# Moving eight weight-difference instructions forward, and one block's second layer by one slot, in a fused gated-recurrence and maxout kernel

## The chip, the cores and the metric

The kernel runs on one core of one Trainium2 chip. Five engines work side by side, each with its own in-order instruction stream: PE (TensorE, matrix products), DVE (VectorE), ACT (ScalarE), POOL (GpSimd) and SP (which only issues transfers here). They wait for one another through semaphores. Time is the device time of one execution in microseconds (us). The kernel before takes 382.12 us, the median of 7 runs that lie between 382.0 and 382.54.

## The reference

Two stages are computed, one after the other. The first is a gated recurrence over 6144 time steps, for 4 batches and 256 channels. The second treats all 24576 tokens as rows and passes them through a layer of 1024 units, where each unit takes the larger of two products, and then through an output projection.

```python
sig = 1.0 / (1.0 + np.exp(-f_logit))
f = lower_bound + (1.0 - lower_bound) * sig
for t in range(S):
    h = f[:, t] * h + (1.0 - f[:, t]) * x[:, t]
    y[:, t] = h
tokens = y.reshape(B * S, D)                  # 24576 x 256
g = np.maximum(tokens @ w1, tokens @ w2)      # 24576 x 1024
out = g @ w_out                               # 24576 x 256
```

## The kernel before

**Algebra.** max(a, b) is written as a + ReLU(b - a). So with `wd` = w2 - w1 (scaled by the gate's factor) the first layer is ReLU(y @ wd), and the rest of the maximum, y @ w1 @ w_out, becomes one small extra product with `w13` = w1 @ w_out. The output is then ReLU(y wd) @ w_out + y @ w13: for each group of 128 tokens ten products, two with `w13` and eight with `wob` (w_out in fp16).

**Blocks and pairs.** Tokens are cut into 48 blocks of 512 time steps; two neighbouring blocks are a pair, so pair 2 is blocks 4 and 5 and pair 3 is blocks 6 and 7. For each block DVE computes the decay (`decay`, line 213), the drive (`drive`, line 223) and two scans along time (`scan`, line 230), one for each half of the channels; ACT computes the gate's sigmoid (`gate`, line 207, or `pair_gate`, line 285).

**First layer.** `first_layer(j, fc)` is two matrix products of 128x128 by 128x512 on PE (line 436) for one eighth of the hidden units. Two such calls, an even and an odd `fc`, fill one PSUM tile `dT`; the odd call is followed by one ReLU on ACT (line 444) that empties it into `r`. There are two `dT` tiles, so PE can be at most two of them ahead of ACT.

**Second layer, plain form.** Blocks 0 to 3 and the last two take `second_layer(j, slot)`: 40 products (line 482) for a block, issued in eight groups of five. After the groups 3 and 7 a PSUM tile is full and is copied out (line 496); for blocks 1 to 3 that copy is on DVE. After group 7 the store to memory is queued on SP (line 455).

**Second layer, seven products.** All other pairs use a scheme with seven products instead of eight for the two blocks of a pair (`sevenths`, matrix products on line 605). It needs four sums of ReLU tiles, made on DVE for each pair (`sum_of`, line 506: `sum3`, `sum1`, `sum2`, `sum4`), and four fixed differences of the weights, t1 to t4. `make_sevens` gives these as eight DVE subtractions (line 415): for each of t1, t3, t2, t4 in this order one of 128x512 from `wob` and one of 128x128 from `w13`.

**Order by hand.** The schedule is manual: the order of calls in the program is the order on every engine. Ahead of the main loop, blocks 0 to 3 are worked off in loops over `fc`. In the main loop each pair has 16 slots. A slot issues one `first_layer`, then (in pair 2 only) possibly one group of `second_layer(3, ...)`, then (from slot 2 of pair 3 on) a share of the queue of `sevenths` products of the pair before, then in slot 2 the transposing transfers of a later chunk (`cross`, SP and POOL), then in some slots a gate on ACT, and last those DVE steps of the list `seq` whose number is below 9 times (slot + 1). In pair 2 `seq` holds the two late scans of block 5 (27, 36), decay, drive and scans of block 6 (64 to 84), the eight subtractions (100 to 114), `sum3` (112), and decay and drive of block 7 (131, 133). In pair 3 it begins with `sum1` (9), `sum2` (18), the scans of block 7 (27, 36) and `sum4` (50).

**What the first products wait for.** In pair 3 the `sevenths` queue starts with 20 products that need only `r`, then 20 that read the result of `sum1` and t1, then 20 that read `sum2` and t2. The first layer of block 7, slot 8 of pair 3, needs the two scans of block 7.

Of the kernel before, what the change touches and what calls it, by code (L numbers as in the profile page):

```python
# [18 lines left out]
def kernel(  # L19
# [25 lines left out]
    for b in range(B):  # L45
# [3 lines left out]
        for nt in sizes:  # L49
            first = len(blocks)  # L50
# [45 lines left out]
    def fetch(c, s):  # L96
        b, t0, nt, _ = chunks[c]
        src = srcs[s][b, t0 : t0 + nt, :]
        if by_xbar(c, s):
            nc.gpsimd.dma_start(  # L100
                out=pieces(scratch[s][c % NSCR][:]), in_=pieces(src)
            )
        else:
            nat = inpool.tile([P, TB // P, D], HALF, name=("fT", "xT")[s])
            nc.gpsimd.dma_start(
                out=nat[:].rearrange("p i d -> p (i d)"),
                in_=src.rearrange("(p i) d -> p (i d)", p=P),
            )
            held[c, s] = nat
# [3 lines left out]
    def fetch_first(k):  # L113
        nt = TB // 2
        for s in range(2):
            raw = opool.tile([P, nt // P, D], FP32, name="osb")
            nc.sync.dma_start(
                out=raw[:],
                in_=srcs[s][0, k * nt : (k + 1) * nt, :].rearrange(
                    "(p i) d -> p i d", p=P  # L120
                ),
            )
            raws[k, s] = raw
# [215 lines left out]
    def fetch_w(g):  # L339
        cols = slice(g * DFF // NG, (g + 1) * DFF // NG)  # L340
        for w, src in ((w1n, moe_w1), (w2n, moe_w2)):
            nc.sync.dma_start(
                out=w[g][:],
                in_=src[:, cols].rearrange("(kc p) f -> p kc f", p=P),
            )

    def pool_waits(t):
        nc.gpsimd.tensor_copy(out=waited[:], in_=t)  # L348
# [56 lines left out]
    def right(k, cols):  # L405

        return wob[:, k * KH : (k + 1) * KH, cols], w13[:, k, cols]

    def make_sevens():
        b11, b12, b21, b22 = (right(k, c) for k in range(2) for c in (lo, hi))  # L410
        parts = [(t[:, 0:KH, :], t[:, KH, :]) for t in (t1, t2, t3, t4)]

        def minus(out, a, b):
            return [
                lambda q=q: nc.vector.tensor_tensor(  # L415
                    out=out[q], in0=a[q], in1=b[q], op=ALU.subtract
                )
                for q in range(2)
            ]

        return [
            *minus(parts[0], b12, b11),
            *minus(parts[2], b22, b12),
            *minus(parts[1], b22, parts[0]),
            *minus(parts[3], b21, parts[1]),
        ]
# [85 lines left out]
    def sum3(p):  # L512
        sum_of(p, 3, quarter(p, 0, 0), quarter(p, 1, 0), ALU.subtract)
# [105 lines left out]
    with tc.manual_schedule():  # L619
        nc.sync.dma_start(out=lbc[:], in_=lower_bound.rearrange("(h p) -> p h", p=P))  # L620
        nc.vector.tensor_copy(out=ident[:], in_=ident_f[:])
        nc.vector.tensor_scalar(
            out=om[:], in0=lbc[:], scalar1=-1.0, scalar2=1.0, op0=ALU.mult, op1=ALU.add
        )
        nc.vector.tensor_scalar_add(out=nom[:], in0=lbc[:], scalar1=-1.0)
        fetch_first(0)
        fetch_first(1)
        for g in range(NG):
            fetch_w(g)
        pool_waits(w1n[0][:, 0, 0:1])  # L630
        nc.gpsimd.dma_start(
            out=wob[:].rearrange("p (g q) c -> p g (q c)", g=NG),
            in_=moe_w_out.rearrange("(g p q) c -> p g (q c)", g=NG, q=NQ),
        )
        for c in range(1, 6):
            for s in range(2):
                fetch(c, s)
        nc.scalar.activation(out=warm[:], in_=om[:, 0:1], func=AF.Sigmoid)
        wt = ps_d.tile([P, 2, 2 * TB], HALF, name="dT")
        for q in range(8):  # L640
            nc.tensor.transpose(wt[:, 0, 0:P], ident[:], ident[:])
        first_bf16(0, 0, nc.vector.tensor_copy)
        first_bf16(0, 1, nc.vector.tensor_copy)
        first_turn(0)
        first_recurrence(0)
        first_bf16(1, 0, nc.scalar.copy)
        first_bf16(1, 1, nc.scalar.copy)
        first_turn(1)
        first_recurrence(1)
        for q in range(24):  # L650
            nc.tensor.transpose(wt[:, 0, 0:P], ident[:], ident[:])
        scale_w1(0)
        half_w1(0, nc.scalar.copy)
        make_wd(0)
        pt = turn_w1(0)
        keep_w1T(0, pt)
        scale_w1(1)
        for fc in range(4):
            first_layer(0, fc)
        half_w1(1, nc.vector.tensor_copy)  # L660
        make_wd(1)
        pt = turn_w1(1)
        for fc in range(4, 8):
            first_layer(0, fc)
        keep_w1T(1, pt)
        steps = turn_steps(1)
        make_w13(0)
        turn(steps[:8])
        gate(1)
        make_w13(1)  # L670
        turn(steps[8:])
        for step in scan_steps(1):
            step()
        cross(4, 5)
        for fc in range(FC):
            if fc == 4:
                turn(turn_steps(2))
                gate(2)
            second_layer(0, fc)
        for step in scan_steps(2):  # L680
            step()
        for fc in range(FC):
            first_layer(1, fc)
        turn(turn_steps(3))
        gate(3)
        early = scan_steps(3)
        for fc in range(FC):
            first_layer(2, fc)
            second_layer(1, fc)
            if fc < 4:  # L690
                early[fc]()
        cross(6)
        scans = {PAIR0: pair_scans(PAIR0)}
        gates = {0: 0, 1: 1, 4: 2, 5: 3}
        order = {
            2: ("decay0", "drive0"),
            3: ("scan00",),
            4: ("scan01",),
            6: ("decay1",),
            7: ("drive1",),  # L700
        }
        for fc in range(FC):
            first_layer(3, fc)
            second_layer(2, fc)
            if fc in gates:
                pair_gate(PAIR0, gates[fc])
            for t in order.get(fc, ()):
                scans[PAIR0][t]()

        queue, due = [], 0  # L710
        for p in range(PAIR0, NPAIR):
            first = p == PAIR0
            more = p + 1 < NPAIR
            seq = [(27, scans[p]["scan10"]), (36, scans[p]["scan11"])]
            if more:
                scans[p + 1] = pair_scans(p + 1)
                seq += [
                    (64, scans[p + 1]["decay0"]),
                    (66, scans[p + 1]["drive0"]),
                    (70, scans[p + 1]["scan00"]),  # L720
                    (84, scans[p + 1]["scan01"]),
                    (112, lambda: sum3(p)),
                    (131, scans[p + 1]["decay1"]),
                    (133, scans[p + 1]["drive1"]),
                ]
            if first:
                seq += [(100 + 2 * n, step) for n, step in enumerate(make_sevens())]
            else:
                seq += [
                    (9, lambda: sum1(p - 1)),  # L730
                    (18, lambda: sum2(p - 1)),
                    (50, lambda: sum4(p - 1)),
                ]
                queue += sevenths(p - 1)
            seq.sort(key=lambda e: e[0])
            gates = {4: 0, 6: 1, 12: 2, 14: 3} if more else {}
            for slot in range(2 * FC):
                first_layer(2 * p + slot // FC, slot % FC)
                if first and slot % 2 == 0:
                    second_layer(2 * p - 1, slot // 2)  # L740
                if p > PAIR0 + 1 or (p == PAIR0 + 1 and slot >= LAG):
                    due += NSEV / (2 * FC)
                    while due >= 1:
                        due -= 1
                        queue.pop(0)()
                if slot == 2 and p + 3 < NPAIR:
                    cross(blocks[2 * p + 6][3])
                if slot in gates:
                    pair_gate(p + 1, gates[slot])
                while seq and seq[0][0] < (slot + 1) * 9:  # L750
                    seq.pop(0)[1]()
        for step in queue:
            step()
        for j in (NBLK - 2, NBLK - 1):
            for slot in range(FC):
                second_layer(j, slot)
# [30 lines left out]
```

## Time and profile before

| what | value |
|---|---|
| median of 7 runs | 382.12 us |
| the profiled execution, its own time | 382.19 us |
| span of that execution in the profile | 380.4 us, so 1.8 us lie around it |
| PE busy | 369.4 us, 97% of the span |
| DVE busy | 332.9 us, 88% |
| ACT busy | 300.4 us, 79% |
| granted TensorE clock | full in all 40 slices |

The page lists, for each engine, busy time, the idle time in front of its instructions, and which engine's instruction ended that idle time (the releaser). The chain that ended last is followed back from the last instruction: at each step to what released it, or to the instruction before it on the same engine. A timeline row gives the start, the time from the first start to the last end, the engine, the line and the operation, and in brackets the idle time before it. Instructions overlap a little on one engine: the distance from start to start is shorter than the duration given. Times of the trace are microseconds from the start of the span.

### The profile page before, as it was taken

What the parts mean: (1) busy time and instruction counts of PE and PEld (TensorE: products, weight loads), DVE (VectorE), ACT (ScalarE), POOL (GpSimd) and SP (SyncE); (2) the same over time, 40 slices, a digit from 0 to 9 for tenths busy, and PEclk for the clock granted to TensorE, in tenths of its full rate; (3) what the DMA queues carried; (4) which work ended last, traced back from release to release, by engine and by line L of the source; (5) the groups of instructions that cost most, each with busy time, mean ns of one, the idle gap of its engine ahead of it and who ended that gap; (6) DMA issues with size and microseconds to landing.
All of it is one profiled execution on the core that took longest, in us unless ns stands there. A gap on an engine that the chain in (4) does not pass through costs nothing.

```text
span 380.4 us, 9454 instructions
## 1 busy us (share of the span) xinstructions
PE 369.4 (97%) x4076; PEld 280.0 (74%) x4076; DVE 332.9 (88%) x402; ACT 300.4 (79%) x406; POOL 38.9 (10%) x79
## 2 busy tenths in 40 slices
PE   4999998999999999999999999999999999999995
PEld 3677766777777777777777777777777777777784
DVE  5685789999999999999999999999999999999721
ACT  5856787798788888888887987988888888888740
POOL 1500111210101101101001202001101101100000
PEclk9999999999999999999999999999999999999999
DMA  7996989999999999999999999999999999940223
GB/s 252 249 221 146 294 163 196 253 201 177 190 169 261 177 215 235 176 216 236 187 243 262 215 189 264 155 247 211 237 226 258 202 209 215 236 193 4 110 113 113
DMA packets 103389, 77.17 MB, mean 203 GB/s; under 512 B 93554, under 2 KB 94066, under 8 KB 102642
## 3 DMA queue, kind: packets, MB, share of 16 engines
q1 hardware_dynamic: 100514, 51.13, 61.0%
q0 software_dynamic: 2544, 25.17, 34.6%
q8 instruction: 32, 0.52, 0.5%
q10 hardware_dynamic: 288, 0.26, 0.2%
q14 instruction: 11, 0.09, 0.1%
HBM read 53.48 MB, written 48.23 MB: 267 GB/s over the span
## 4 chain that ended last, share of the span: by engine, by line
PE 91%; DVE 5%; DMA 1%; ACT 1%; SPq 0%; issue 0%
PE ps L605 42%; PE dT L436 41%; PE ps L482 6%; DVE r L230 1%; DVE S L506 1%; DMA osb<-in_f_logit_dram 1%; PE ps L180 1%; DVE wd L360 1%; DVE t L415 0%; DVE v L223 0%; PE ps L392 0%; DVE ff L213 0%; DVE osb L496 0%; DVE r L264 0%; ACT r L444 0%
## 5 line engine op out<-in xcount | busy, mean ns | idle before, releaser
L444 ACT ACTIVATE r<-dT 128x1024 f16<-128x1024 f32 x192 | 195.8, 1023 | 55.3 <-PE dT L436 55.2
L436 PE MATMUL dT<-r,wd 128*128 128x512 f16 x768 | 225.8, 379 | 1.1 <-ACT r L444 0.5
L605 PEld LDWEIGHTS <-S 128*128 128x128 f16 x1680 | 110.9, 101 | 38.6 <-DVE S L506 1.2
L605 PEld LDWEIGHTS <-r 128*128 128x128 f16 x1260 | 87.3, 101 | 36.6
L230 DVE TENSOR_TENSOR_SCAN r<-ff,r,v 128x512 f16<-128x512 f16 x88 | 108.2, 1271 | 0.8
L605 PE MATMUL ps<-t,S 128*128 128x128 f16 x1260 | 97.8, 219 | 1.0 <-DVE S L506 1.0
L436 PEld LDWEIGHTS <-wd 128*128 128x128 f16 x768 | 67.6, 113 | 6.8 <-issue 1.2
L506 DVE TENSOR_TENSOR S<-r 128x2560 f16<-128x2560 f16 x42 | 62.5, 1488 | 10.4 <-ACT r L444 10.3
L605 PE MATMUL ps<-wob,r 128*128 128x128 f16 x672 | 67.4, 219 | 0.0
L506 DVE TENSOR_TENSOR S<-r,S 128x2560 f16<-128x2560 f16 x42 | 62.0, 1477 | 0.0
L285 ACT ACTIVATE u<-fT 128x512 f16<-128x512 f16 x88 | 56.0, 637 | 0.0
L348 POOL CAST waited<-fT 128x1 f32<-128x1 f16 x21 | 12.6, 600 | 280.3 <-DMA fT<-scr 280.3
L213 DVE TENSOR_SCALAR ff<-u,nom 128x512 f16<-128x512 f16 (+1 forms) x98 | 31.4, 346 | 10.9 <-ACT u L207 6.7
L605 PE MATMUL ps<-w,r 128*128 128x128 f16 x168 | 36.8, 219 | 0.0
L562 DVE TENSOR_TENSOR osb<-ps,sn 128x512 f32<-128x512 f32 x42 | 28.7, 684 | 6.5 <-ACT osb L560 5.3
L605 PE MATMUL ps<-t,r 128*128 128x128 f16 x420 | 33.4, 219 | 0.0
L605 PE MATMUL ps<-wob,S 128*128 128x128 f16 x336 | 31.4, 219 | 0.0
L223 DVE TENSOR_TENSOR v<-u,xT 128x1024 f16<-128x1024 f16 x44 | 30.2, 686 | 0.0
L482 PEld LDWEIGHTS <-r 128*128 128x128 f16 x240 | 23.9, 101 | 6.9
L482 PE MATMUL ps<-wob,r 128*128 128x256 f16 x192 | 26.8, 273 | 0.0
L550 ACT COPY sn<-ps 128x512 f32<-128x512 f32 x42 | 24.6, 586 | 1.1 <-PE ps L605 1.1
L560 ACT COPY osb<-ps 128x512 f32<-128x512 f32 x42 | 24.4, 581 | 0.5 <-PE ps L605 0.5
(56 smaller groups left out, 135.0 us busy)
## 6 DMA issues: line engine op xcount, KB each, us to landing
out_dram<-osb SPq DMA_DIRECT2D x47, 512.0 KB, 3.8
scr<-in_f_logit_dram POOLq DMA_DIRECT2D x22, 512.0 KB, 7.4
scr<-in_x_dram POOLq DMA_DIRECT2D x22, 512.0 KB, 10.3
r<-in_moe_w_dram SPq DMA_DIRECT2D x4, 512.0 KB, 6.6
fT<-in_f_logit_dram POOLq DMA_DIRECT2D x3, 256.0 KB, 8.0
xT<-in_x_dram POOLq DMA_DIRECT2D x3, 256.0 KB, 8.7
osb<-in_f_logit_dram SPq DMA_DIRECT2D x2, 256.0 KB, 4.2
osb<-in_x_dram SPq DMA_DIRECT2D x2, 256.0 KB, 3.7
```

The source lines that it names most:

```text
L213: nc.vector.tensor_scalar(out=ff[:, h, cols], in0=u[:, h, cols], scalar1=nom[:, h : h + 1], scalar2=1.0, op0=ALU.mult, op1=ALU.add,)
L223: nc.vector.tensor_tensor(out=like(v[:, :, cols], xT), in0=like(u[:, :, cols], xT), in1=xT, op=ALU.mult,)
L230: nc.vector.tensor_tensor_scan(out=y_of(j, h), data0=ff[:, h, o : o + TB], data1=v[:, h, o : o + TB], initial=0.0 if t0 == 0 else y_of(j - ...
L285: nc.scalar.activation(out=mids[p + NBLK, "u"][:, h, cols], in_=held[c, 0][:, h, cols], func=AF.Sigmoid, scale=-1.0,)
L436: nc.tensor.matmul(dT[:, fc % 2, :], lhsT=wd[:, kc, unit_cols(fc)], rhs=y_of(j, kc), start=(kc == 0), stop=(kc == KC - 1),)
L444: nc.scalar.activation(out=rts[j, k][:, g - 1 : g + 1, :].rearrange("p q (i m) -> p q i m", m=P), in_=dT[:].rearrange("p q (m i) -> p q i ...
L482: nc.tensor.matmul(ps[:, r, :], lhsT=left, rhs=right, start=(s == 0 and (r == 0 or j == NBLK - 1)), stop=(s == n - 1 and (r == 1 or j == N ...
L506: nc.vector.tensor_tensor(out=t[:], in0=a, in1=b, op=op)
L550: nc.scalar.copy(out=t[:], in_=bank[b][:])
L560: nc.scalar.copy(out=dst, in_=bank[b][:])
L562: nc.vector.tensor_tensor(out=dst, in0=bank[b][:], in1=snap[name][:], op=ALU.add)
L605: nc.tensor.matmul(bank[b][:, i, :], lhsT=a[:, k, cols], rhs=w, start=fresh, stop=after is not None, skip_group_check=True,)
```

## The change

The list of eight subtractions is taken out of `seq` of pair 2 and issued ahead of the main loop, directly behind the decay, drive and scans of block 2, before the first layer of block 1. In pair 2, the eight groups of the second layer of block 3 stand in slots 1, 3, ... 15 instead of 0, 2, ... 14. Everything else, and the work as a whole, is as before.

```diff
         for step in scan_steps(2):
             step()
+        for step in make_sevens():
+            step()
         for fc in range(FC):
             first_layer(1, fc)
         turn(turn_steps(3))
...
-            if first:
-                seq += [(100 + 2 * n, step) for n, step in enumerate(make_sevens())]
-            else:
+            if not first:
                 seq += [
                     (9, lambda: sum1(p - 1)),
...
                 first_layer(2 * p + slot // FC, slot % FC)
-                if first and slot % 2 == 0:
+                if first and slot % 2:
                     second_layer(2 * p - 1, slot // 2)
```

## The prediction

> **What bounds the kernel.** I read the busy shares first, then the chain that ended last in order of time, then the idle times of PE and DVE around the change.
>
> ```profile
> PE 369.4 (97%) x4076; PEld 280.0 (74%) x4076; DVE 332.9 (88%) x402; ACT 300.4 (79%) x406; POOL 38.9 (10%) x79
> PE 91%; DVE 5%; DMA 1%; ACT 1%; SPq 0%; issue 0%
> ```
>
> PE is the bound as a whole, so only time in which PE stands still, on the path, can be won. The chain says where that is. From 29 us on it runs through PE alone, except for one stretch (columns: start, length, what):
>
> ```profile
> 49.62 0.56 PE ps L482 x5
> 50.18 0.02 issue
> 50.20 0.69 DVE osb L496
> 50.90 0.53 DVE ff L213 x2
> 51.42 0.61 DVE v L223
> 52.03 0.03 issue
> 52.06 2.46 DVE r L230 x2
> 54.52 1.40 DVE t L415 x6
> 55.91 1.40 DVE S L506
> 57.32 0.47 DVE t L415 x2
> 57.79 0.60 DVE osb L496
> 58.39 0.53 DVE ff L213 x2
> 58.91 0.60 DVE v L223
> 59.51 2.81 DVE S L506 x2
> 62.32 2.38 DVE r L230 x2
> 64.70 0.04 issue
> 64.74 0.38 PE dT L436
> ```
>
> For 14.5 us, from the copy of block 3's first half (line 496, released by group 3 of its second layer at 50.18) to the scans of block 7, DVE has no idle time, and PE at 64.74 waits for its last scan. The eight subtractions (L415) stand in this stretch. What PE loses there is in its timeline, in brackets:
>
> ```profile
> 57.39 0.59 PE L436 MATMUL dT<-r,wd 128*128 128x512 f16 x2 [0.29 <-ACT r L444]
> 60.97 0.51 PE L605 MATMUL ps<-t,S 128*128 128x128 f16 x6 [1.01 <-DVE S L506]
> 64.74 0.38 PE L436 MATMUL dT<-r,wd 128*128 128x512 f16 x1 [0.30 <-DVE r L230]
> ```
>
> The first waits for a `dT` tile that ACT empties, the second for `sum1`, the third for the last scan of block 7. Together 1.60 us. After 64.74 PE's timeline shows no idle time up to the end. So 1.60 us is all that an edit here can win, and what is won at 64.74 is kept unless a new wait appears.
>
> **The subtractions leave the full stretch.** In the chain they take 1.40 (six of them) and 0.47 (two): 1.87 us, which every later DVE step in the stretch gets back. Here a rule and the row differ. The Trainium skill, "VectorE: DVE Perf Modes", section "Side-by-side: where the cycles go for N=2048 bf16", counts for a 16-bit operation at two elements per cycle N/2 + 8 + about 150 cycles at 0.96 GHz: an estimate of 0.43 us for 512 elements and 0.23 for 128, so 4 x 0.43 + 4 x 0.23 = 2.65 us. That is near the durations in the trace (0.40 to 0.42 and 0.22), but one starts before the one ahead has ended (54.44, 54.75, 54.89, 55.22), so start to start is 0.33 and 0.14. I take 1.87. By the rule the stretch would shorten by 2.65 and DVE would no longer be last; PE's own 1.60 would then be the gain.
>
> **Where they go.** Behind the scans of block 2, DVE stands idle:
>
> ```profile
> 24.84 2.46 DVE L230 TENSOR_TENSOR_SCAN r<-ff,r,v 128x512 f16<-128x512 f16 x2
> 30.44 0.62 DVE L213 TENSOR_SCALAR ff<-u,nom 128x512 f16<-128x512 f16 x2 [3.14 <-ACT u L207]
> ```
>
> From 27.3 to 30.4 it waits for the gate of block 3 on ACT. The operands are there: `wob` was read by PE from 16.3 us, and the copies of `w13` on ACT began at 17.5 and 18.8. So 1.87 us (2.65 by the rule) fit in 3.14 and cost nothing; 1.27 remain. Without this cover the cost would fall on block 3: its second scan ends at 34.06 + 1.28 = 35.34 and its first layer starts near 37.1, so another 1.7 us are spare before PE stands still. Queued behind the subtractions on DVE is only the decay of block 3. They issue no transfer and pass nothing on SP. On POOL a rule would speak against the move: "SBUF — State Buffer", section "SBUF: two separate sides", says that a DVE operation with two SBUF inputs and a GpSimd operation that reads SBUF lock each other out. The old place shows something like it: POOL's one-column copy at 55.96 took 1.87 us, against 0.18 in many pairs. In the new place POOL has no instruction from 18.0 to 42.3 us, so by the row it costs 0; if a lock of that size did meet it, 1.87 + 1.7 us would still lie almost within the 3.14 + 1.7 of cover.
>
> **The second layer of block 3, one slot later.** A first-layer call is 0.43 us of PE in the chain, a group of five 0.55. The order in pair 2 becomes two first-layer calls, one group, and so on: the same products and alternation, one call shifted. Three effects follow.
>
> First, group 3 now comes behind eight calls instead of seven. The copy that starts the DVE stretch moves from 50.18 to 50.61: a loss of 0.43. Block 5's first layer in slot 8 starts behind the same eight calls and four groups as before.
>
> Second, PE no longer issues three first-layer calls in a row at the boundary (slot 15, then slots 0 and 1 of pair 3, at 55.64), the cause of the 0.29. After the change slot 15 ends at 44.96 + 16 x 0.432 + 7 x 0.549 = 55.71. ACT then still has a gate: the ReLU of slot 13 starts at 54.3, the gate follows at 55.2, and the ReLU of slot 15 starts near 55.8 and ends near 56.8. PE returns to that tile at 44.96 + 18 x 0.432 + 8 x 0.549 = 57.13. The 0.29 goes, with about 0.3 to spare.
>
> Third, the second copy of block 3 moves from slot 14 to slot 15, so on DVE behind decay and drive of block 7 instead of ahead. Its group ends near 56.1 and DVE reaches it at 57.5, so it waits for nothing. Its store on SP stands behind transposing transfers that SP issues from 63.62 to 69.2, before and after. Nothing changes there.
>
> **The sum.** DVE's stretch starts 0.43 later and is 1.87 shorter: its end comes 1.44 earlier. Step by step from 50.63: copy, decay, drive and scans 4.32 to 54.95; `sum3` to 56.35 (its ReLU of slot 11, from FL end 52.9, is done near 54.0); decay, drive, copy 1.73 to 58.08 (the gate of slot 14 is done near 55.9); `sum1` to 59.48; `sum2` to 60.88; scans to 63.26. PE reaches the `sum1` products at 60.97 - 1.01 - 0.29 = 59.67, when `sum1` is just there. It reaches block 7's second product at 64.44 - 1.30 = 63.14 and waits until 63.30: 0.16 of the 1.60 remain. The gain is 1.44 us. From there PE, DVE and ACT stand to one another as before. Against the profiled execution: 382.19 - 1.44 = 380.75, span near 379.0; that execution is 0.07 above the median, so the forecast is 382.12 - 1.44 = **380.7 us**, 0.38% faster. 0.2%, or 0.76 us, is about what a measurement of this kernel can tell from no change.
>
> **Rivals.** *PE's own limit.* If the subtractions give back more than 1.87, or group 3 comes sooner, DVE is early and all of 1.60 goes: 380.5. For it: the margins are 0.06 and 0.16. Against: the chain measures the 1.87. Chance 0.14.
>
> *DVE waits where it now never does.* With the subtractions gone it reaches `sum3` 0.9 us sooner, and the gated decay of block 7 1.9 us sooner than before. The margins worked out above are 0.9 and 0.5 us. If ACT is late there by 0.5 us more than these, the gain is 0.94: 381.2. Chance 0.11.
>
> *The change doesn't pay because the feed doesn't follow.* The transfers through the scratch buffers run in their own loop.
>
> ```profile
> 55.96 1.87 POOL L348 CAST waited<-fT 128x1 f32<-128x1 f16 x1 [12.10 <-DMA fT<-scr]
> 60.48 0.63 ACT L285 ACTIVATE u<-fT 128x512 f16<-128x512 f16 x1
> ```
>
> The first row is the landing of the chunk whose first gate is the second: 4.5 us ahead, the least of the pairs I compared (another is 160.19 against 165.24). Were the margin gone, PE would stand still later for what it won: 382.1. Against: 1.44 leaves 3 us. Chance 0.07.
>
> *Slower: ACT at the `dT` tiles of pair 2.* PE returns to a tile 0.55 + 0.86 + 0.55 = 1.96 us after filling it; a ReLU there ends 1.05 after, or 1.28 with a gate ahead of it, so 0.68 is spare. If the shifted slots made each of the eight ReLUs later than this, each tenth beyond costs PE 0.8 us. It cancels the gain at 0.18 beyond, and makes the kernel measurably slower from 0.28 beyond (8 x 0.28 = 2.2 = 1.44 + 0.76): a ReLU 0.96 later than computed. Priced at 0.35 beyond: 2.8 - 1.44 = 1.4 slower, 383.5. Only the wait at 57.39 speaks for it. Chance 0.08.
>
> **Chances and range.** The likeliest has 0.60 and its own range is 380.5 to 381.0 (the spread of the runs shown, and a tenth or two in the sum). Faster by over 0.2%: 0.60 + 0.14 + 0.11 = 0.85. Within 0.2%: 0.07. Slower: 0.08. The range leaves out the last two rivals, 0.15, and takes in the first two: from 380.5 less 0.3 of spread to 381.2 plus 0.4, so 380.2 to 381.6.
>
> **What would show it.** In the changed profile: eight L415 rows from 27.3 to 29.2 and the decay of block 3 still at 30.44 behind the gate; the copy L496 near 50.6; no idle before the product near 57.1; at most a tenth before the first L605 product that reads `S` (near 59.7); a remaining wait of about 0.16 for the scan near 63.3; no PE idle after it. A PE wait for ACT between 45 and 57, a DVE wait ahead of `sum3` or the decay near 56.4, or a gate that waits for a transfer would make the prediction wrong.

## The result, and the profile after

The changed kernel takes 380.70 us (median of 13 runs, 380.44 to 382.25) against 382.16 for the kernel before (median of 33 runs). The ratio is 0.9963, with a 95% interval from 0.9956 to 0.9970: 0.37% faster. The forecast was 380.7 us. The execution that was profiled took 380.57 us, with a span of 378.7. Some executions of both kernels lie a microsecond or more above their medians (one of the kernel before took 431.14 us, and no profile shows why).

The chain that ended last, in order of time, over the stretch that the prediction read (columns: start, length, what):

```profile
49.78 0.56 PE ps L482 x5
50.34 0.02 issue
50.36 0.69 DVE osb L496
51.06 0.52 DVE ff L213 x2
51.58 0.61 DVE v L223
52.19 0.03 issue
52.22 2.46 DVE r L230 x2
54.68 1.38 DVE S L506
56.06 0.53 DVE ff L213 x2
56.59 0.60 DVE v L223
57.19 0.60 DVE osb L496
57.79 2.80 DVE S L506 x2
60.59 2.38 DVE r L230 x2
62.97 0.04 issue
63.01 0.38 PE dT L436
```

The stretch is still full and PE still waits at its end, but L415 is gone from it. It was 14.5 us long (50.20 to 64.70) and is 12.6 now (50.36 to 62.97).

The trace starts differ by a few tenths from run to run, since the first loads land at different times. So I measure from a fixed point, the first product of block 2's first layer. In the chain it stands here before,

```profile
29.32 0.43 PE dT L436 x2
```

and here after:

```profile
29.05 0.43 PE dT L436 x2
```

From there the copy L496 starts after 20.88 us before and after 21.31 now: 0.43 later. PE's wait for the scan ends after 35.42 before and after 33.96 now: 1.46 earlier. The end of the span comes after 351.08 before and 349.65 now: 1.43 earlier. (A profile gives its span to a tenth, so differences of such sums, here and below, are good to about 0.1 us.) What is won at the end of the stretch is kept to the last instruction.

PE's timeline from the fixed point to the end has one bracket left of the three:

```profile
63.01 0.38 PE L436 MATMUL dT<-r,wd 128*128 128x512 f16 x1 [0.30 <-DVE r L230]
```

And DVE, where the subtractions went:

```profile
24.57 2.46 DVE L230 TENSOR_TENSOR_SCAN r<-ff,r,v 128x512 f16<-128x512 f16 x2
26.95 0.40 DVE L415 TENSOR_TENSOR t<-wob 128x512 f16<-128x512 f16 x1
...
28.67 0.22 DVE L415 TENSOR_TENSOR t<-w,t 128x128 f16<-128x128 f16 x1
30.17 0.62 DVE L213 TENSOR_SCALAR ff<-u,nom 128x512 f16<-128x512 f16 x2 [1.27 <-ACT u L207]
```

The idle time ahead of the decay of block 3 shrank from 3.14 to 1.27 us, by exactly 1.87, and ACT still ends it.

One thing does not fit. The prediction had PE's room at 1.60 us (0.29, 1.01 and 0.30) and a remaining wait of 0.16. The bracket still says 0.30, as before, though the other two are gone: 1.30 less waiting is shown, but 1.46 was won.

### The profile page after: what moved, and what is told of

It reads as the page before. It is cut to its first block, busy times and chain, and to the rows that moved or that the text cites. A ratio compares the mean times of both kernels' runs of the same rounds, so it can differ in the third digit from the quotient of the medians.

```text
span 378.7 us, 9454 instructions
## 1 busy us (share of the span) xinstructions
PE 368.4 (97%) x4076; PEld 279.4 (74%) x4076; DVE 332.9 (88%) x402; ACT 300.5 (79%) x406; POOL 38.8 (10%) x79
## 4 chain that ended last, share of the span: by engine, by line
PE 91%; DVE 4%; DMA 1%; ACT 1%; SPq 1%; issue 0%
PE ps L605 43%; PE dT L436 41%; PE ps L482 6%; DMA r<-in_moe_w_dram 1%; DVE r L230 1%; DVE S L506 1%; DVE wd L360 1%; PE ps L180 1%; PE ps L392 0%; SPq L117 0%; ACT r L352 0%; DVE osb L496 0%; DVE v L223 0%; DVE ff L213 0%; ACT r L444 0%; DVE S L356 0%
```

## The experiments

Two readings of PE's brackets were set against each other. Reading A takes them as they stand. Reading B comes from looking again at how PE's rows follow one another in the changed kernel:

```profile
56.66 0.59 PE L436 MATMUL dT<-r,wd 128*128 128x512 f16 x2
57.09 0.39 PE L605 MATMUL ps<-wob,r 128*128 128x128 f16 x4
57.32 0.22 PE L605 MATMUL ps<-w,r 128*128 128x128 f16 x1
57.37 0.33 PE L605 MATMUL ps<-wob,r 128*128 128x128 f16 x3
```

Two products of 512 columns take 0.43 us until the next may start, 0.216 each, and four of 128 take 0.23, or 0.057 each. The length of a single one is shown as 0.38 and 0.22. So a product lets the next start about 0.16 us before its shown end, and a bracket, which begins at the shown end, leaves out 0.16 us of each wait. The Trainium skill, "TensorE: Matmul & The Clock Gate", section "Back-to-back issue gap", has the same two spacings, 56 and 216 ns, for isolated products at full clock. For a stream of weight loads and products, which this kernel is, it has about 81 and 131 ns instead; the rows here show the first pair, and they decide. By reading B the waits before were 0.45, 1.17 and 0.46: a room of 2.08 us.

### The subtractions alone

```diff
-                if first and slot % 2:
+                if first and slot % 2 == 0:
```

(against the changed kernel)

> Only the eight subtractions move; the second layer of block 3 stays in the even slots. Two readings of PE's waits are compared. Reading A takes the three idle times of the profile before as they stand (0.29, 1.01 and 0.30 us). The wait of 0.29 us for ACT stays, the other two go, since DVE is 1.87 us earlier: gain 1.31 us, 380.85 us against 382.16. Reading B says that each bracket counts from the modelled end of the last product, and that the next product could have started about 0.16 us before that end, so that the waits are 0.45, 1.17 and 0.46 us: gain 1.17 + 0.46 = 1.63 us, 380.53 us, a little more than the whole change.

It took 380.53 us against 382.15 (ratio 0.9961, interval 0.9946 to 0.9976). From the fixed point (29.17) to the end of the span (378.6) there are 349.43 us: 1.65 less than before. Reading B said 1.63, reading A 1.31. PE's only bracket behind the fixed point is the one for ACT:

```profile
57.24 0.59 PE L436 MATMUL dT<-r,wd 128*128 128x512 f16 x2 [0.29 <-ACT r L444]
```

So the first half of the change alone gains all that the whole change does. In the whole change, the move to the odd slots takes away this wait and pays for it with a later start of the DVE stretch.

### The odd slots alone

```diff
-                if first and slot % 2 == 0:
+                if first and slot % 2:
```

(against the kernel before)

> Only the second layer of block 3 moves to the odd slots; the subtractions stay in pair 2. The theory of the full DVE stretch: it starts one first-layer call later and is as long as before, so its end, and all after it, comes 0.43 us later: 382.59 us against 382.16. The rival, that the wait of 0.29 us for ACT at the start of pair 3 counts for itself: up to 0.45 us faster, 381.7 us.

It took 382.63 us against 382.15 (ratio 1.0016, interval 1.0007 to 1.0025): slower by 0.48. The wait for ACT is gone, and the one for `sum1` has grown:

```profile
62.30 0.51 PE L605 MATMUL ps<-t,S 128*128 128x128 f16 x6 [1.88 <-DVE S L506]
66.07 0.38 PE L436 MATMUL dT<-r,wd 128*128 128x512 f16 x1 [0.30 <-DVE r L230]
```

1.88 and 0.30, each with 0.16 more, are 2.50 against 2.08 before: 0.42 lost. The wait for `sum1` grew by 0.87: the 0.45 that PE no longer waits for ACT, and the 0.42 by which DVE is later. From the fixed point (30.23) to the end of its span (381.7) it is 351.47, 0.39 more than before. Where DVE is full, a wait of PE that is taken away in front of it goes into PE's next wait for DVE.

### Even slots, then odd ones

```diff
-                if first and slot % 2:
+                if first and slot % 2 == (slot >= FC):
```

(against the changed kernel)

> The subtractions as in the change; the groups 0 to 3 of block 3's second layer in the slots 0, 2, 4, 6 (so the DVE stretch starts as early as before), the groups 4 to 7 in the slots 9, 11, 13, 15 (so the wait for ACT goes). The end of the DVE stretch comes 1.87 us earlier. Reading A of the waits: PE's whole room is 1.60 us, gain 1.60, 380.56 us. Reading B: PE's room is 2.08 us, DVE sets the end, gain 1.87 us, 380.29 us, with 0.05 us of idle time shown ahead of the second product of block 7's first layer (0.21 us of loss).

It took 380.61 us (380.07 to 381.97 over 8 runs) against 382.15, ratio 0.9963, interval 0.9950 to 0.9976. Its runs spread too widely to tell the readings apart by time. The profile does: 349.16 us from the fixed point (29.64) to the end (378.8), 1.92 less than before, where B said 1.87 and A 1.60. No bracket is left behind the fixed point, yet a loss is there. The two products of slot 8 in pair 3, the second of which awaits block 7's last scan, are spread:

```profile
62.24 0.67 PE L605 MATMUL ps<-t,S 128*128 128x128 f16 x9
62.74 0.79 PE L436 MATMUL dT<-r,wd 128*128 128x512 f16 x2
63.37 0.61 PE L605 MATMUL ps<-t,S 128*128 128x128 f16 x8
```

Two such products span 0.59 where nothing is awaited: 0.20 us of waiting, against 0.21 worked out, that no list of waits shows as PE's. (Of the 0.20, 0.16 are hidden; the 0.04 left are too short for a bracket, the smallest of which in these timelines is 0.15.)

### A copy moved to ACT as well

```diff
-                (nc.scalar.copy if j == 0 else nc.vector.tensor_copy)(
+                (nc.scalar.copy if j == 0 or (j, i) == (3, 3) else nc.vector.tensor_copy)(
```

(against the kernel of the last experiment)

> As the kernel before this one, and the copy of the second half of block 3 is made by ACT instead of DVE, which takes 0.60 us more out of the DVE stretch, so that PE's own room is the limit. Reading A: gain 1.60 us, 380.56 us, the same as without the copy on ACT. Reading B: gain 2.08 us, 380.08 us, and no idle time of PE in pairs 2 and 3. A third outcome: the copy delays ACT's ReLU at the start of pair 3 (0.5 us of work more) and PE waits there for a dT tile, so that some of it is lost again.

380.69 us (379.95 to 381.76 over 6 runs) against 382.15, ratio 0.9960, interval 0.9945 to 0.9976: by time, undecided. By the profile 348.96 us from the fixed point (30.64) to the end (379.6), 2.12 less than before: reading B's 2.08, with PE's rows in pair 3 at their usual spacing and no bracket. Reading A would have stopped at 1.60. The third outcome didn't come: ACT's ReLU behind the copy ran without a wait of PE for it.

It was run again beside the changed kernel.

> The changed kernel itself, run beside the next three on one chip so that they can be set against it: 380.7 us against 382.15.

> The kernel with the mixed slots and the second copy of block 3 on ACT once more, beside the changed kernel on one chip. In the profiles the time from the first product of block 2's first layer to the end of the span was 351.08 us before, 349.65 with the change and 348.96 here. If that is the whole difference, this kernel is 0.6 to 0.7 us ahead of the change, 380.05 us. If the run-to-run spread of the start-up (27 to 31 us) hides it, the intervals overlap.

The changed kernel: 380.80 us (ratio to before 0.9961, interval 0.9951 to 0.9971). This one: 380.11 us (0.9942, interval 0.9921 to 0.9963). From the fixed point it is 349.03 us again (29.27 to 378.3). The difference of 0.69 us is what the profiles say (0.62 with this profile, 0.69 with the one ahead of it); the intervals still overlap.

### How much cover the new place has

```diff
-        for step in make_sevens():
+        for step in 2 * make_sevens():
```

(against the changed kernel; the same values are written again)

> The changed kernel with the eight subtractions issued twice in their new place, so with 1.87 us more of DVE work there. If the cover is as worked out (3.14 us of idle time and 1.7 us before the first layer of block 3 needs the scans), the decay of block 3 starts 0.6 us later and nothing comes later: 380.7 us. With the price of the skill's page (2.65 us for eight) the decay would be 2.2 us late and the end 0.5 us: 381.2 us.

380.77 us, beside 380.80 of the changed kernel on the same chip. DVE's rows:

```profile
27.31 0.40 DVE L415 TENSOR_TENSOR t<-wob 128x512 f16<-128x512 f16 x1
...
30.92 0.22 DVE L415 TENSOR_TENSOR t<-w,t 128x128 f16<-128x128 f16 x1
31.05 0.62 DVE L213 TENSOR_SCALAR ff<-u,nom 128x512 f16<-128x512 f16 x2
```

Sixteen take 31.05 - 27.31 = 3.74 us, twice 1.87, and not twice the 2.65 that the prediction worked out from the Trainium skill ("VectorE: DVE Perf Modes", "Side-by-side: where the cycles go for N=2048 bf16"). The gap is used up. The decay starts at once behind the subtractions, 1.63 us from the fixed point (29.42) against 1.12 in the changed kernel: 0.5 us later, where 0.6 was expected. The end doesn't move, since the second cover holds.

> The same with the subtractions issued four times: 7.48 us of DVE work in the gap of 3.14. The decay of block 3 starts 4.3 us late, 1.7 of it are cover, PE waits 2.6 us for the scan ahead of the first layer of block 3, and everything behind comes 2.6 us later: 380.7 + 2.6 = 383.3 us. If the gap's size did not matter, because other work on DVE gives way later, the time would stay at 380.7; if the second cover did not exist, 385.0.

With `4 * make_sevens()`: 383.22 us against 382.21 (ratio 1.0035, interval 1.0022 to 1.0049), 383.3 expected. PE waits for the two scans of block 3:

```profile
37.70 0.41 PE L436 MATMUL dT<-r,wd 128*128 128x512 f16 x1 [0.76 <-DVE r L230]
39.47 0.38 PE L436 MATMUL dT<-r,wd 128*128 128x512 f16 x1 [1.36 <-DVE r L230]
```

The brackets add up to 2.12. With 0.16 for each it is 2.44. The fixed point here is 29.11 (the first product at 28.95 on PE's timeline, 0.16 earlier than the chain counts it, as in the other profiles), so 352.09 us to the end of the span (381.2): 2.44 more than the changed kernel's 349.65. This fits reading B once more, in another place of the kernel and with the opposite sign.

### More output buffers

The profiled execution of the changed kernel in its second run took 382.42 us, 1.6 above its median. PE had a wait there that no other profile of these kernels has:

```profile
219.23 0.27 PE L605 MATMUL ps<-t,r 128*128 128x128 f16 x2 [1.25 <-DVE osb L562]
```

and DVE's timeline has the reason:

```profile
218.48 0.69 DVE L562 TENSOR_TENSOR osb<-ps,sn 128x512 f32<-128x512 f32 x1 [1.99 <-DMA out_dram<-osb]
```

A store to memory had not yet freed its output buffer. It was issued at 204.44 and took 12.7 us to land. The longest landing of a store in the other profiles is 11.3 to 13.8 us, without such a wait, so its length alone does not explain the stop. Two kernels with six such buffers instead of four were run:

```diff
-    opool = ctx.enter_context(tc.tile_pool(name="opool", bufs=4))
+    opool = ctx.enter_context(tc.tile_pool(name="opool", bufs=6))
```

> The changed kernel with six output buffers (the pool opool) instead of four. In one profile of the changed kernel, of an execution of 382.42 us, PE stood still for 1.25 us at 219.23, because DVE and ACT waited 2.0 and 2.3 us for a store to free an output buffer. If such late stores are what puts some executions 1.3 to 1.7 us above the rest (4 of 22 of the changed kernel lay above 381.5), they go and all runs lie within 0.8 us, with the same median of 380.7 us. If something else makes them, about one in five stays above 381.5.

> The kernel with the mixed slots and the second copy of block 3 on ACT, also with six output buffers: 380.05 us, 0.65 us ahead of the changed kernel with six output buffers on the same chip, if the difference of the profiles (348.96 against 349.65 us from the first layer of block 2 on) is the whole difference; and no run more than 0.8 us above the rest if late stores make the slow ones.

The changed kernel with six buffers: 380.61 us (380.45 to 380.73 over 5 runs; ratio to before 0.9960, interval 0.9946 to 0.9974). The kernel with mixed slots and the copy on ACT, with six buffers: 380.11 us (379.84 to 380.28; ratio 0.9947, interval 0.9935 to 0.9959). The second is 0.5 us ahead, its highest run below the lowest of the first, and 349.03 against 349.63 us from the fixed point to the end. No execution of either was late, but on that chip none of the 9 of the kernel before was either (highest 382.43), so whether the buffers help stays open.

## Why the prediction was right

**The size.** 1.44 us was forecast, 1.46 was measured at the end of the stretch and 1.43 at the end of the span. The sum was made along DVE: 1.87 out of the stretch, 0.43 lost by its later start. Both terms are in the profile as worked out, and each half was run alone.

**The new place is free.** The decay of block 3 still starts when ACT's gate is done. The two covers, 3.14 and 1.7 us, were tested with twice and four times the work, and the cost at four times, 2.44 us in the profile, was expected at 2.6.

**Rule and row.** The price by the skill's rule (2.65 us) is near the sum of the rows' lengths, but what counts between rows is the distance of their starts: 1.87 for eight and 3.74 for sixteen. The row was the right choice. The other rule, that DVE and POOL can lock each other out, met nothing in the new place: POOL has no instruction between 18.7 and 42.5 us in the profile after. POOL's side of it fits the profile before: its copy at 55.96 ends at 57.83, just behind the last subtraction (57.79), and one at 69.89 ends at 71.12, just behind a sum on DVE (71.08). What DVE would lose by it, no run here tests.

**The step that was mis-sized.** "So 1.60 us is all that an edit here can win" is wrong, and with it "0.16 of the 1.60 remain". PE's room was 2.08 us, since each of the three brackets hides 0.16 of its wait. After the change 0.62 remain: 0.46 at the scan (shown as 0.30), and 0.16 ahead of the first product that reads `sum1`, which starts at 59.24, 0.22 behind a product that lets the next start after 0.057:

```profile
59.02 0.22 PE L605 MATMUL ps<-w,r 128*128 128x128 f16 x1
59.24 0.51 PE L605 MATMUL ps<-t,S 128*128 128x128 f16 x6
```

This second wait is in no bracket. The forecast survived because DVE, whose terms were taken from start to start, was the one that set the end, and because the error lay on the harmless side: the room is larger than was worked out. Had PE's own limit set the end, the sum would have been 0.48 short. The rival "PE's own limit" gave 380.5 us; the kernels that reach that limit are at 380.1, and 2.05 to 2.12 us in the profile.

**The other rivals.** The wait of DVE for late ReLUs or gates didn't come: between the copy at 50.36 and the scans its rows have no idle time. Late ReLUs at the `dT` tiles of pair 2 didn't come either: PE's wait for ACT at 57.39 is gone and none has come in its place. The prediction laid that wait to calls that follow one another, slot 15 and slots 0 and 1. PE still issues three in a row after the change (0, 1 and 2, from 55.80), but a group of 0.55 us now lies between slot 15 and slot 2, which takes the tile of slot 15 again. A gate did wait for a transfer, which the prediction had named as a sign against it:

```profile
37.78 0.63 ACT L285 ACTIVATE u<-fT 128x512 f16<-128x512 f16 x1 [0.39 <-DMA fT<-scr]
```

That is ACT's first gate of pair 2, ahead of the place where time was won. The ReLU behind it starts at 38.38, 9.33 us from the fixed point, as before (38.65, the same 9.33), so it cost nothing, and this sign was too strict. The margin of the feed that the prediction followed, 4.5 us at the first gate of pair 4, is now 2.5 (landing at 57.24, gate at 59.76).

**Which half did it.** The odd slots are worth nothing beside the subtractions: 380.53 without them and 380.70 with them, which the times alone can't tell apart. The profiles (349.43 against 349.65) go against them, as do the waits that are left: 0.45 without them, 0.62 with them. They take a wait of 0.45 us from PE and start DVE's full stretch 0.43 us later.

## What to carry to other kernels

When one engine is full over a stretch and the bound engine waits for it at the end, make the sum along the full engine, from the event that starts the stretch to the wait at its end, and let no more than the bound engine's room count. Moving work out of such a stretch into a gap gains its start-to-start time; a wait of the bound engine that is removed within it comes back at the bound engine's next wait for the full one, until that one is relieved. (The second half of this rests on the run of the odd slots alone: to take the wait for ACT away, without a later start of the stretch and with the subtractions in their old place, was not tried.) And size the room by the distance of starts, against the usual distance of such rows, not by the brackets.

## What the runs showed of the hardware that was not expected

The profile shows the idle time in front of a pipelined product 0.16 us too small. It was seen on products of 128 and of 512 columns, at waits for DVE and for ACT, and waits below 0.16 us are not shown as idle at all. With the smallest bracket at 0.15, a wait of PE under about 0.31 us has none.

The store of an output tile can be late enough to stop PE: in one execution DVE and ACT waited 2.0 and 2.3 us for it and PE lost 1.25 + 0.16 us. The cause of the late store was not settled.

It is not the cause of every late execution. Two others that were profiled, 383.60 us (the odd slots alone) and 381.41 (the first run with the copy on ACT), lost their time before the fixed point, which stands at 30.23 and 30.64 there and at 29.05 to 29.64 in the other profiles; behind it they are as expected. Part of it lies in the first eight products of the first layer. They took 2.99 and 3.49 us in these two (from 12.25 and 12.17), but 2.29 before and 2.16 with the change; the next eight took 1.89 in both. What made them slow was not tried out.
